# Second matmul of the channel MLP as seven block products (Strassen, Winograd's form) instead of eight, with the steps of all groups placed anew

## The chip, the cores and the metric

The kernel runs on one core of a Trainium2 chip. The metric is device time in microseconds. Three runs of the kernel before gave 284.55, 285.14 and 286.96 us; the median, 285.14, is the time before.

## The reference

Attention with pooled keys and values, then an MLP mixer with residuals, cut to its core:

```python
k_p = k.reshape(B, H, Sp, 8, D).mean(axis=3)          # B 8, H 8, S 576, D 64, Sp 72
v_p = v.reshape(B, H, Sp, 8, D).mean(axis=3)
attn = softmax(scale * q @ k_p.T)
x = (attn @ v_p) as (B, S, 512)
h = np.maximum(x.T @ w_tok1, 0.0) @ w_tok2            # tokens: 576 -> 256 -> 576
u = x + h.T
h2 = np.maximum(u @ w_ch1, 0.0) @ w_ch2               # channels: 512 -> 1536 -> 512
return u + h2                                         # float32
```

## The kernel before, in words

Five engines each work through a queue of their own in the order in which the program writes the instructions: TensorE (PE), VectorE (DVE), ScalarE (ACT), GpSimd (POOL), SyncE (SP, stores). Semaphores hold an instruction back until its data and its buffer are there; nothing else ties a queue to another.

**Groups.** The channel MLP is done in nine groups of 512 tokens. Groups 0 to 7 are the first 512 tokens of batches 0 to 7; group 8 is the remaining 64 tokens of all eight batches ("tails"). For one group `unit_steps` writes 12 hidden tiles m (4 matmuls of 512 columns each, L438, then a ReLU on ScalarE into GT, L442), and then 4 output tiles c (12 matmuls of 512 columns each, L461, then an addition of u on VectorE, L466, and two stores on SP, L469). In group 8 the last output tile is cut into two halves of 256 columns (L450, L453, L455). A `yield` after every two matmuls makes some 48 numbered steps of a group.

**The rest, woven in.** Attention and token mixing of the following batches are cut into small named pieces, and the tables FIRST, SECOND, THIRD and LATER (L476 to L488) say after which step of a group each piece is written. The pieces are those of batch n+1, with ">" of batch n+2, with "<" of batch n:

- K0, K1, V0, V1: pooling of half of the heads' keys or values on GpSimd; k0, k1, v0, v1: the same on VectorE. Each is `pool8` (L142), three additions of two SBUF tiles (L145, L146, then L149 for keys or L151 for values).
- lk, lq, lv: loads, issued by GpSimd. Q0 to Q3: transposes of q on VectorE (L243). kpT: four TensorE transposes of the pooled keys (L194) and a copy on VectorE (L196).
- s0 to s3: scores, 8 small matmuls (L254) and two exponentials on ScalarE (L260). av0 to av4: attention times values, 8 matmuls (L292), then a reciprocal and a product on VectorE (L304, L310).
- at0, at1: first token matmul, 5 matmuls (L338) and a ReLU on ScalarE or VectorE (L329, L331). u0 to u4: second token matmul, 2 or 4 matmuls (L353) and the addition of x on VectorE (L354).
- u must be transposed for the next group's hidden tiles: t0 to t4 do so on TensorE (L363, copy L364 on VectorE); M0, M2, M4, M and T0 to T4 do it through memory, by two DMA steps on SP (L372, L379) and a block transpose on VectorE (L385).

Batch 0 is prepared in a head (HEAD) ahead of group 0.

**PSUM.** Eight banks: three single ones (`ps_one`, "p1"), two double ones (`ps_two`, "p2", scores and av) and one for transposes (`ps_tr`, "pt"). A tile that takes over a bank waits for the readers of the one before.

## Time and profile before

| what | value |
|---|---|
| median of three runs | 285.14 us |
| span of the profiled execution, first to last instruction | 283.7 us (no other time of this execution is given) |
| end of HEAD, start of group 0 | about 24.7 us |
| group 0 | 24.7 to 63.4 us |
| groups 3, 4, 5 | 28.1, 29.0, 28.1 us |
| group 7, from the first hidden tile to the first of group 8 | 238.4 to 259.1 us |
| ReLU of a hidden tile, L442 | 0.596 us |
| output addition of 512 columns, L466 | 0.682 us |
| GpSimd busy, all ahead of 176 us | 138.1 us |

In the profile a line such as L438 is a line of the kernel; PEld is the loading of weights, which overlaps PE. In the chain of work that ended last, each piece is followed back to what released it; it tells which engine set the end. In the timeline, the columns are start, length, engine, line, operation and tiles, and in brackets the idle time of the engine ahead of it and what ended it. The granted clock of TensorE is 0.993 over the span; it is lower only in one slice of group 0.

### The profile page before, as it was taken

Reading aid. Unit: us, or ns where it says so; the run is one execution under the profiler, and the core shown is the slowest. Engines: PE = TensorE matmul, PEld = TensorE weight load, DVE = VectorE, ACT = ScalarE, POOL = GpSimd, SP = SyncE. Lnnn points to the kernel's source line nnn. Section 1 sums busy time; section 2 is a strip of 40 time slices with the busy share of each in tenths; the row PEclk is TensorE's granted clock in tenths of the full one; section 3 lists DMA queues with packets and bytes.
Section 4 is the critical chain, followed back from the end, with each engine's and each line's share of the span. In section 5 each row is a group of like instructions: output and inputs, shape, how many; then the busy total and the mean of one; then the engine's idle time right before and its main releaser. Section 6 shows DMA issues by size and latency. Waiting matters only on the chain.

```text
span 283.7 us, 4529 instructions
## 1 busy us (share of the span) xinstructions
PE 273.8 (97%) x1816; PEld 130.9 (46%) x1816; DVE 149.4 (53%) x279; ACT 110.2 (39%) x193; POOL 138.1 (49%) x124
## 2 busy tenths in 40 slices
PE   8999879999999999999999999999999999999994
PEld 3855325443544445354435443544354444444443
DVE  5466975679657557474648464746474243011012
ACT  2543554009602643514561356135613511612600
POOL 8684993999999929973993696000000000000000
PEclk9999979999999999999999999999999999999999
DMA  7999999951982397159748964514242346015014
GB/s 158 193 202 208 204 202 186 217 121 40 124 138 64 74 127 126 37 78 200 162 75 137 231 165 52 112 39 122 45 96 55 102 64 136 16 37 112 2 39 109
DMA packets 36837, 32.68 MB, mean 115 GB/s; under 512 B 14288, under 2 KB 30288, under 8 KB 36816
## 3 DMA queue, kind: packets, MB, share of 16 engines
q0 software_dynamic: 18672, 17.64, 40.0%
q1 hardware_dynamic: 17984, 14.62, 21.8%
q8 instruction: 14, 0.23, 0.3%
q10 hardware_dynamic: 160, 0.13, 0.2%
q14 instruction: 7, 0.06, 0.1%
HBM read 38.21 MB, written 11.80 MB: 176 GB/s over the span
## 4 chain that ended last, share of the span: by engine, by line
PE 91%; DVE 5%; ACT 2%; issue 1%
PE p L461 31%; PE p L438 31%; PE p L353 6%; PE p L338 5%; PE p L254 4%; PE p L292 3%; PE pt L495 3%; ACT ex L260 2%; DVE qD L243 1%; PE pt L363 1%; DVE t L145 1%; PE p L450 1%; PE p L272 1%; PE p L321 1%; PE p L403 1%; PE p L225 1%
## 5 line engine op out<-in xcount | busy, mean ns | idle before, releaser
L461 PE MATMUL p<-w_ch,GT 128*128 128x512 bf16 x420 | 102.3, 380 | 0.0
L442 ACT ACTIVATE GT<-p 128x512 bf16<-128x512 f32 x108 | 64.3, 596 | 80.6 <-PE p L438 80.5
L438 PE MATMUL p<-uT,w_ch 128*128 128x512 bf16 x384 | 95.5, 382 | 0.0
L438 PEld LDWEIGHTS <-w_ch 128*128 128x128 bf16 x432 | 40.2, 98 | 47.9 <-issue 4.8
L461 PEld LDWEIGHTS <-GT 128*128 128x128 bf16 x420 | 37.6, 98 | 41.2 <-issue 3.5
L260 ACT ACTIVATE ex<-p 72x576 bf16<-72x576 f32 x56 | 33.1, 642 | 28.4 <-PE p L254 28.4
L145 POOL TENSOR_TENSOR t<-kr 72x1024 f32<-72x1024 bf16 x13 | 27.5, 2118 | 26.6 <-DMA kr<-in_k_dram 25.9
L466 DVE TENSOR_TENSOR o<-p,u 128x512 f32<-128x512 f32 x32 | 21.8, 682 | 32.3 <-PE p L461 32.2
L146 POOL TENSOR_TENSOR t<-t 72x512 f32<-72x512 f32 x25 | 33.3, 1332 | 2.0
L354 DVE TENSOR_TENSOR u<-p,x 128x512 bf16<-128x512 f32 x32 | 22.1, 691 | 13.7 <-PE p L353 13.7
L145 POOL TENSOR_TENSOR t<-vr 72x1024 f32<-72x1024 bf16 x12 | 25.5, 2123 | 0.8
L385 DVE STREAM_TRANSPOSE uT<-v 128x512 bf16<-128x512 bf16 x16 | 10.4, 685 | 22.0 <-DMA v<-mem 22.0
L310 DVE TENSOR_TENSOR x<-p,den 128x512 bf16<-128x512 f32 x30 | 20.7, 692 | 1.0
L243 DVE STREAM_TRANSPOSE qD<-qb 128x576 bf16<-128x576 bf16 x28 | 20.5, 789 | 0.0
L329 ACT ACTIVATE AT<-p 128x512 bf16<-128x512 f32 x8 | 4.8, 597 | 39.3 <-PE p L338 36.6
L292 PEld LDWEIGHTS <-ex 72*128 72x128 bf16 x320 | 15.4, 98 | 9.9 <-DVE x L310 0.8
L353 PE MATMUL p<-AT,w_tok 128*128 128x512 bf16 x64 | 19.0, 379 | 0.0
L292 PE MATMUL p<-vp,ex 72*128 72x65 bf16 x320 | 16.8, 194 | 0.5 <-DVE x L310 0.3
L254 PE MATMUL p<-qD,kD 32*72 32x288 bf16 x224 | 14.5, 306 | 2.0 <-DVE kD L196 1.8
L304 DVE RECIPROCAL den<-p 128x8 f32<-128x8 f32 (+1 forms) x39 | 8.0, 204 | 13.6 <-PE p L292 13.0
L338 PE MATMUL p<-x,w_tok 128*128 128x512 bf16 x56 | 14.4, 380 | 0.0
L331 DVE TENSOR_SCALAR AT<-p 128x512 bf16<-128x512 f32 x8 | 5.5, 692 | 13.7 <-PE p L338 12.9
(88 smaller groups left out, 207.3 us busy)
## 6 DMA issues: line engine op xcount, KB each, us to landing
out_dram<-o SPq DMA_DIRECT2D x70, 128.0 KB, 2.4
kr<-in_k_dram POOLq DMA_DIRECT2D x7, 576.0 KB, 8.7
qb<-in_q_dram POOLq DMA_DIRECT2D x7, 576.0 KB, 11.9
vr<-in_v_dram POOLq DMA_DIRECT2D x7, 576.0 KB, 15.1
w_ch<-in_moe_w_ch_dram POOLq DMA_DIRECT2D x6, 512.0 KB, 13.2
mem<-u SPq DMA_DIRECT2D x8, 256.0 KB, 2.1
v<-mem SPq DMA_DIRECT2D x8, 160.0 KB, 3.7
v<-mem SPq DMA_DIRECT2D x8, 128.0 KB, 3.4
```

Of the source, the lines that this page charges most:

```text
L145: eng.tensor_tensor(out=t4[:, 0:n], in0=t[:, hs, 0:4], in1=t[:, hs, 4:8], op=ALU.add)
L146: eng.tensor_tensor(out=t4[:, 0:n, 0:2], in0=t4[:, 0:n, 0:2], in1=t4[:, 0:n, 2:4], op=ALU.add)
L243: nc.vector.transpose(out=late("qD")[:, g, db].rearrange("m (r j u) -> m u r j", u=2, r=BR), in_=st["qraw"][:, g].rearrange("m (u r d) -> ...
L254: nc.tensor.matmul(out=pss[l // 2][0:SP, l % 2, 0:SH], lhsT=st["kD"][quad, g, db, :], rhs=st["qD"][quad, g, db, half * SH:(half + 1) * SH] ...
L260: nc.scalar.activation(out=exv[:, h:h + 2], in_=pss[a][0:SP, :, 0:SH], func=AF.Exp, scale=scale)
L292: nc.tensor.matmul(out=halves[h // 4][:, (h % 4) * (D + 1):(h % 4 + 1) * (D + 1)], lhsT=st["ex"][:, h * S + n0:h * S + n0 + P], rhs=st["vp ...
L338: nc.tensor.matmul(out=ps, lhsT=w_tok1[:, c if c < 4 else 4 + par, m * P:(m + 1) * P], rhs=st["x"][:, c, :] if c < 4 else st["xt"], start= ...
L353: nc.tensor.matmul(out=ps, lhsT=w, rhs=a, start=(i == 0), stop=(i == len(mms) - 1))
L354: nc.vector.tensor_tensor(out=dst, in0=ps, in1=x, op=ALU.add)
L438: nc.tensor.matmul(out=ps, lhsT=w_ch1[:, kk, m * P:(m + 1) * P], rhs=uT[:, kk, :], start=(kk == 0), stop=(kk == 3))
L442: nc.scalar.activation(out=GT[:, m, :], in_=ps, func=AF.Relu)
L461: nc.tensor.matmul(out=ps, lhsT=GT[:, m, c * P:(c + 1) * P], rhs=w_ch2[:, m, :], start=(m == 0), stop=(m == NM - 1))
```

## The change

The second matmul of a group (512 tokens, 1536 hidden, 512 channels) is cut in two along each of its sizes: A11 to A22 of GT (a half of the tokens by a half of the hidden channels), B11 to B22 of w_ch2. It is computed from seven block products instead of eight. A product has 12 matmuls of 256 columns. Products 1, 2, 3 and 4 take at least one plain block, products 5, 6 and 7 take mixed ones: `S1` = A21 + A22, `S2` = S1 - A11, `S3` = A11 - A21, `S4` = A12 - S2 for the activations (`g_mix`, new in each group), and four mixes of the weights (`w_mix`, `W1` to `W4`, once, in group 0). They are written in the order 1, 2, 5, 6, 4, 3, 7. Products 1, 6 and 7 add up in one PSUM bank ("x"), 5 and 3 in another ("z"), 2 and then 4 each have one ("y"). Each of the four output quarters is read from two of these banks at different moments, by a first join (which adds u) and a second.

New names in the tables: S1 to S4 mix on VectorE and G1 to G4 on GpSimd ("a" and "b" mean the first and the second half of the hidden channels); C1a to C4b are joins on VectorE, D a drain of a bank to SBUF on ScalarE with E, the addition of u on GpSimd, in place of a first join. "=" means this group, "-" the one before, whose last joins run in the next group. Each group has a table of its own, and all pieces have new steps. New variants of pieces: kpA and r0 to r4 are kpT and t0 to t4 with the copy on ScalarE, aw0 to aw4 are av with the normalisation on ScalarE (eight instructions like L307), ax0 and ax1 are at with the ReLU on ScalarE; at0 now has it on VectorE.

A hidden group is written in the order of ORDER, so that both halves grow together. There are now 24 hidden steps and 21 product steps of four matmuls. PSUM has four single banks for all that was in `ps_one` and `ps_tr`. w_ch2 is loaded in four quarters, an output quarter is stored in two pieces with rows of 256 channels, and some tiles of the head share their SBUF with g_mix.

The diff, cut to its core:

```diff
-    ps_one = ctx.enter_context(tc.tile_pool(name="ps_one", bufs=3, space=bass.MemoryType.PSUM))
+    ps_one = ctx.enter_context(tc.tile_pool(name="ps_one", bufs=4, space=bass.MemoryType.PSUM))
     ps_two = ctx.enter_context(tc.tile_pool(name="ps_two", bufs=2, space=bass.MemoryType.PSUM))
-    ps_tr = ctx.enter_context(tc.tile_pool(name="ps_tr", bufs=1, space=bass.MemoryType.PSUM))
...
+    HM, HN, HT = NM // 2, DM // 2, 2 * P
+    w_mix = [w_ch2[:, 0:HM, HN:DM] if i == 2 else singles.tile([P, HM, HN], BF16, name=f"w_mix{i}") for i in range(4)]
+    g_mix = []
+
+    def early(i, shape, dtype):
+        return shared.tile(shape, dtype, name=f"shared{i}")
...
-    def load_ch2(gs):
-        for g in gs:
-            nc.gpsimd.dma_start(out=w_ch2[:, 4 * g:4 * g + 4, :],
-                                in_=moe_w_ch2[g * 512:(g + 1) * 512, :].rearrange("(c p) n -> p c n", p=P))
+    def load_ch2():
+        for j in range(2):
+            for i in range(2):
+                nc.gpsimd.dma_start(out=quad(w_ch2, i, j), in_=moe_w_ch2[i * HM * P:(i + 1) * HM * P, j * HN:(j + 1) * HN]
+                                    .rearrange("(c p) n -> p c n", p=P))
...
-        def kpT():
-            ps = ps_tr.tile([P, 4, SP], BF16, name="pt")
+        def kpT(eng):
+            def go():
+                transpose_keys(eng)
+            return go
+
+        def transpose_keys(eng):
+            ps = ps_one.tile([P, 4, SP], BF16, name="p1")
             for i in range(4):
                 nc.tensor.transpose(out=ps[:, i, :], in_=st["kp"][:, i // 2, i % 2].rearrange("j l d -> j (l d)"),
                                     identity=ident[0:SP, 0:SP])
-            nc.vector.tensor_copy(out=st["kD"].rearrange("p g e j -> p (g e j)"), in_=ps.rearrange("p i j -> p (i j)"))
+            eng(out=st["kD"].rearrange("p g e j -> p (g e j)"), in_=ps.rearrange("p i j -> p (i j)"))
...
+    def quad(t, i, j):
+        return t[:, i * HM:(i + 1) * HM, j * HN:(j + 1) * HN]
+
+    def mix_weights(i):
+        b11, b12, b21, b22 = quad(w_ch2, 0, 0), quad(w_ch2, 0, 1), quad(w_ch2, 1, 0), quad(w_ch2, 1, 1)
+        a, b = ((b12, b11), (b22, w_mix[0]), (b22, b12), (b21, w_mix[1]))[i]
+        nc.vector.tensor_tensor(out=w_mix[i], in0=a, in1=b, op=ALU.subtract)
...
+            self.bank, self.o = {}, {}
+            if not g_mix:
+                g_mix.extend(early(i, [P, HM, HT], BF16) for i in range(4))
...
+        def a(self, i, j):
+            return self.GT[:, j * HM:(j + 1) * HM, i * HT:(i + 1) * HT]
+
+        def mix(self, eng, i, m0, m1):
+            x, y, op = ((self.a(1, 0), self.a(1, 1), ALU.add), (g_mix[0], self.a(0, 0), ALU.subtract),
+                        (self.a(0, 0), self.a(1, 0), ALU.subtract), (self.a(0, 1), g_mix[1], ALU.subtract))[i]
+            eng.tensor_tensor(out=g_mix[i][:, m0:m1], in0=x[:, m0:m1], in1=y[:, m0:m1], op=op)
+
+        def product(self, i):
+            g, w, b = {1: (self.a(0, 0), quad(w_ch2, 0, 0), "x"), 2: (self.a(0, 1), quad(w_ch2, 1, 0), "y"),
+                       3: (g_mix[3], quad(w_ch2, 1, 1), "z"), 4: (self.a(1, 1), w_mix[3], "y"),
+                       5: (g_mix[0], w_mix[0], "z"), 6: (g_mix[1], w_mix[1], "x"), 7: (g_mix[2], w_mix[2], "x")}[i]
+            new = i in (1, 2, 4, 5)
+            if new:
+                self.bank[b] = ps_one.tile([P, 2, HN], FP32, name="p1")
+            ps = self.bank[b]
+            for k in range(2 * HM):
+                c, m = k // HM, k % HM
+                nc.tensor.matmul(out=ps[:, c, :], lhsT=g[:, m, c * P:(c + 1) * P], rhs=w[:, m, :],
+                                 start=new and k == 0, stop=k == 2 * HM - 1, skip_group_check=True)
+                if k % 4 == 3:
                     yield
...
+        def join(self, q, v, last):
+            u = self.uq(q // 2, q % 2)
+            if not last:
+                self.o[q] = outp.tile([P, 2, HN], FP32, name="o")
+            nc.vector.tensor_tensor(out=self.o[q], in0=self.bank[v], in1=self.o[q] if last else u, op=ALU.add)
+            if last:
+                self.store(q)
+
+        def drain(self, q, v):
+            self.o[q] = outp.tile([P, 2, HN], FP32, name="o")
+            nc.scalar.copy(out=self.o[q], in_=self.bank[v])
+
+        def add_u(self, q):
+            nc.gpsimd.tensor_tensor(out=self.o[q], in0=self.o[q], in1=self.uq(q // 2, q % 2), op=ALU.add)
+
+        def store(self, q):
...
+        def act(self, s):
+            v, g = nc.vector, nc.gpsimd
+            if s[0] == "S":
+                lo, hi = {"": (0, HM), "a": (0, HM // 2), "b": (HM // 2, HM)}[s[2:]]
+                self.mix(v, int(s[1]) - 1, lo, hi)
+            elif s[0] == "G":
+                lo, hi = {"": (0, HM), "a": (0, HM // 2), "b": (HM // 2, HM)}[s[2:]]
+                self.mix(g, int(s[1]) - 1, lo, hi)
+            elif s[0] in "CDE":
+                q, va, vb = {"1": (0, "x", "y"), "2": (1, "x", "z"), "3": (3, "z", "x"), "4": (2, "y", "x")}[s[1]]
+                if s[0] == "D":
+                    self.drain(q, va)
+                elif s[0] == "E":
+                    self.add_u(q)
+                else:
+                    self.join(q, vb if s[2] == "b" else va, s[2] == "b")
+
+    def unit_steps(n):
+        w = units[n] = Unit(n)
+        for m in ORDER:
+            yield from w.hidden(m)
+        for i in (1, 2, 5, 6, 4, 3, 7):
+            yield from w.product(i)
...
+    LAST = "C4a C2b C4b E3 C3b"
+    PLANS = [
+        {0: '<u1', 4: 'k1', 6: 'Q2 Q1 K0 Q0', 8: '<u0 <u3 Q3', 9: 'kpA s1 lv2', 11: 's0', 12: 'v0', 14: '=S1a s2', 16: 'V1 <u2', 17: 's3', 18: '=S2a', 19: 'lq3 W1', 20: 'av0', 21: 'av2', 22: 'av1', 23: '=G3 aw4 >K0', 24: '=S1b av3', 25: 'W2', 26: 'W3 W4 ax0 =D1 ax1', 27: 'u4 u2', 28: 'r4 =S2b =E1', 29: '=C1b u1', 31: 'u3', 32: 'r2', 33: '=S4', 34: 'r1', 35: 'lk3 =C3a u0', 36: '>Q2', 37: 'r3', 38: 'lv3 =D2 >K1', 39: '>V1', 40: '>kpA', 41: '>Q3', 42: 'r0 >s2'},
+        {0: '-C4a >Q3 -E2', 1: 'Q1 >Q1', 2: 'Q0', 3: '-C3b >Q2 s1 V0', 6: '-C4b', 8: 's0 -C2b', 9: 'lv3', 11: '>Q0', 12: 's3 >K1', 13: '>k0', 15: 'av1 lq3', 16: 'av2', 18: 'av0', 19: '=S1a >V1', 20: 'av4', 21: '>V0', 22: 'av3', 23: '=S1b =S2a >kpA', 24: 'at0 >s2', 26: '=C1a ax1 >s0', 27: 'u3', 28: 'u2', 29: '=G3 =S2b', 31: '>s3 =C1b', 32: '=C3a', 33: 'u1 u0', 34: '>s1 t1', 36: '=S4 =C2a', 38: '>av2', 39: 't2 =D4', 40: '>av3', 41: 'r0 r3', 42: '>aw1', 43: 'lk3'},
+        {0: '-C2b >K1 -E4', 2: 'av0', 4: 'av4', 5: '>K0 >Q1 -C3b', 7: '>Q0', 8: '-C4b lk3', 9: '>Q3', 11: 'ax1', 13: 'ax0', 14: '>kpA', 15: '=S1a >Q2', 16: 'u4', 17: '>s3', 18: 'u2', 19: 'lv3', 21: 'u0 u3 =S2a', 23: 'r2 >s0', 24: 't0', 25: 't3 =S1b', 26: 'u1 >s2 >V0', 27: 't4', 29: '=S2b', 30: '=C1a', 31: '>s1 =S3', 32: '=C1b', 33: '>V1', 34: '=C3a =G4', 35: '>aw1 >av4', 36: '=C2a t1', 41: 'lq3', 42: '=C4a >av2', 43: '>aw3'},
+        {2: '-C4b -C2b >Q3', 3: 'av0', 4: '>Q0', 6: '-C3b >Q1', 7: 'ax0', 8: 'at1', 10: '>K0 >Q2 >K1 >kpT', 12: 'u2', 14: 'u1 u0 u3', 15: '>s1', 17: 'lk3 >V0', 18: '=S1a', 19: 'M0 lq3', 24: 'M2 >s0 =S1b', 27: '=S2b M =S2a', 29: '>s3', 30: '=S4', 31: '>V1', 32: '=C1a =C1b', 33: '>s2 T2', 34: 'T0', 35: '=D2 T1', 36: '=C3a >aw3', 38: 'T3 >av1', 39: '=G3', 40: '=C4a lq4', 43: '>aw2'},
+        {0: '-C4b', 1: 'lv2', 2: '-C3b', 3: '>K0 av4 av0', 4: '-E2 >K1', 5: '>kpA >Q1', 7: '>Q2', 8: '>Q0 -C2b', 9: 'lk3 >Q3', 10: 'ax1 >s0 at0', 12: '=S1a >s1', 14: '=S2a', 15: '>V1', 16: 'u4', 17: 'u2', 18: '>s3 u1 lv3', 19: '>V0', 20: 'u3', 21: '>s2 u0', 25: '=S1b >aw1', 27: '=C1a M4 =S2b', 29: '>av3', 30: 'M2', 31: '>av0 =G4', 33: 'M0 M =D3 >aw2', 34: '=S3', 35: '=C1b', 36: '=D2', 38: '=E3 >av4', 40: '=E2 >ax0 T0', 41: 'T1', 42: 'T3', 43: 'T2 >ax1', 44: '=C4a'},
+        {1: '-C2b -C3b', 3: 'u0 >Q3', 7: '-C4b', 8: '>K1 u3', 9: '<T4 u2', 10: 'u1', 11: '>K0', 12: '>Q2', 13: '>kpA', 14: '>Q1 >V0', 17: 'M2 >V1', 19: '>s2', 20: '=S1a', 23: 'M0 >Q0', 24: '>s0 =S2a M =S1b', 28: '=S2b', 29: '=G4 >s1', 30: '=C1a', 31: 'T0 =S3', 32: '=C1b', 33: '>s3', 35: 'T2 =C3a', 36: '=D2', 37: '>aw1', 38: 'T3 T1', 41: '>av4', 43: '=C4a', 44: '=E2 >av2 =C2b'},
+        {2: 'av0', 5: '-C3b av3', 7: 'at1', 9: 'at0', 10: '-C4b', 14: 'u2', 15: 'u0 u3', 16: '=S1a', 18: 'u4 u1', 19: 'M2', 20: 'M4', 24: 'M0', 25: '=G3', 26: '=S2a', 27: '=S1b =S2b', 29: 'M =C1a', 30: '=C1b =G4', 32: '=C3a T2', 36: '=D2', 37: 'T1', 39: '=D4 T0 =E4', 40: '=E2', 43: 'T3'},
+        {0: '-C2b', 4: '-C3b', 10: '-C4b', 20: '=S1a', 24: '<T4', 27: '=S1b =C1a', 28: '=S2b', 31: '=S2a =G3', 33: '=C1b', 35: '=S4', 38: '=C3a', 40: '=D4', 41: '=C2a =E4'},
+        {3: '-C2b', 4: '-C4b', 5: '-C3b', 24: '=S1a', 26: '=S1b', 28: '=S2a', 32: '=S2b =D1 =E1', 33: '=D3 =C1b', 34: '=S4', 35: '=G3', 40: '=C2a'},
...
+    ORDER = (0, 6, 1, 7, 2, 8, 3, 9, 4, 10, 5, 11)
...
+        for n in range(B + 1):
+            unit(n, PLANS[n])
+        for s in LAST.split():
+            units[B].act(s)
```

## The prediction

> **What bounds the kernel now.** I read the page's busy shares first, then the chain that ended last, then the timeline around two places that the change touches.
>
> ```profile
> PE 273.8 (97%) x1816; PEld 130.9 (46%) x1816; DVE 149.4 (53%) x279; ACT 110.2 (39%) x193; POOL 138.1 (49%) x124
> ...
> PE 91%; DVE 5%; ACT 2%; issue 1%
> ```
>
> TensorE sets the time: it is busy for 97% of the span and holds 91% of the chain. VectorE, at 53%, seems to have room. The second matmul can be read in the pieces of the chain for the last two groups:
>
> ```profile
> 248.76 10.36 PE p L461 x48
> ...
> 277.25 2.63 PE p L450 x24
> ```
>
> 48 matmuls of 512 columns take 10.36 us, 215.8 ns each; 24 of 256 columns take 2.63 us, 109.6 ns each. So half the width costs half the time, and the doubled number of weight loads does not show.
>
> The second place is batch 1's key pooling, which VectorE and GpSimd do at the same time (VectorE's rows, then GpSimd's; columns are start, length, instruction):
>
> ```profile
> 29.21 2.73 DVE L145 TENSOR_TENSOR t<-kr 72x1024 f32<-72x1024 bf16 x1
> 31.98 1.64 DVE L146 TENSOR_TENSOR t<-t 72x512 f32<-72x512 f32 x1
> 33.65 0.83 DVE L149 TENSOR_TENSOR kp<-t 72x256 bf16<-72x256 f32 x1
> ```
> ```profile
> 28.75 2.11 POOL L145 TENSOR_TENSOR t<-kr 72x1024 f32<-72x1024 bf16 x1 [3.27 <-DMA kr<-in_k_dram]
> 30.94 2.13 POOL L146 TENSOR_TENSOR t<-t 72x512 f32<-72x512 f32 x1
> 33.15 1.05 POOL L149 TENSOR_TENSOR kp<-t 72x256 bf16<-72x256 f32 x1
> ```
>
> The ends tell it. GpSimd's first add ends at 30.86; VectorE's, which started at 29.21, ends 1.08 us after that, at 31.94. GpSimd's second add then takes 2.13 us instead of the 1.26 of the same form alone (37.25), and ends 1.13 us after VectorE's. **They take turns**: a VectorE instruction with two SBUF inputs lasts until GpSimd's current one is over and then runs for its own length, and the reverse. VectorE's instructions with a PSUM input keep their length beside GpSimd (0.69 us for L354 and L310 throughout). In before only nine VectorE instructions are of the first kind, all ahead of 71 us.
>
> **The change part by part.** The profile gives only the span of its execution, 283.7 us; the median of the runs is 285.14, so 1.4 us lie around it, and I add them at the end.
>
> *The products.* Each group has 84 matmuls of 256 columns instead of 48 of 512: 84 x 109.6 ns = 9.21 us for 10.36, 1.15 us less. The last group had 36 x 215.8 + 24 x 109.6 ns = 10.40 and loses 1.19. Eight groups and the last: **-10.4 us**. The other matmuls (hidden layer, tokens, attention, 14 transposes) keep their number.
>
> *What this is paid with.* Per group VectorE gets up to three full mixes (6 x 256 elements a row, some cut in half), and 8 joins for 4 (a few go to ScalarE and GpSimd); GpSimd gets one or two mixes and up to three adds. Once there are four weight mixes. A join reads PSUM, 0.69 us as L466. For a mix of two bf16 SBUF tiles before has no row. Bounds: f32 adds (0.42 us for 256, 0.69 for 512) lead to 0.96 us for a half mix and 1.76 for a full one; bf16 copies (0.295 for 288, 0.42 for 512, L196 and L364) lead to 0.56 and 0.99. I take the copies, the row of the same type, and keep the adds for the range. A GpSimd mix is 3.2 us (L145: 2.12 for 1024, same type).
>
> The Trainium skill, "VectorE: DVE Perf Modes", section on the perf-mode tiers, puts bf16 tensor_tensor in SBUF at two elements a cycle; the estimate by its 1224 ns for 2048 elements is about 0.56 us for a half mix, and by its f32 rate it would be 0.96; no row of before decides.
>
> By length alone VectorE goes from some 150 to 180 us, below the span. What counts is where the mixes stand: they are all of the kind that takes turns, and GpSimd is busy through group 5.
>
> *Order in the last groups, by group 7.* There is no attention left, so each wait is seen. Count from the first product (before has the same moment here):
>
> ```profile
> 247.93 0.60 ACT L442 ACTIVATE GT<-p 128x512 bf16<-128x512 f32 x1 [0.27 <-PE p L438]
> ...
> 248.59 2.75 PE L461 MATMUL p<-w_ch,GT 128*128 128x512 bf16 x12
> 248.79 0.60 ACT L442 ACTIVATE GT<-p 128x512 bf16<-128x512 f32 x1 [0.27 <-PE p L438]
> ```
>
> The last hidden tile but one is done at -0.06, the last at +0.8. G3 on GpSimd reads only tiles that are there at -0.06 and stands at the head of its queue, whatever its step says: it runs from 0 to 3.2. S1b needs the last tile, asks at 0.8 and lasts until 3.2 + 0.56 = 3.75. Product 5, due after 24 matmuls at 2.63, waits 1.15. Behind S1b on VectorE stand C1a (to 4.5), S2b (5.05) and S2a (5.6); product 6, now due at 5.1, waits for S2a, 0.55. Then C1b, S4 (0.99) and C3a, to 8.0; product 3, due at 6.97, adds to the bank that C3a reads and waits 1.1. Sum 2.8. Without turns all would be ready in time (S2a at 3.4, C3a at 5.8), so the price is the turns alone. Group 6, same count: S1b waits for G3, product 5 loses 1.2, the rest fits. Group 8: E1 waits for the ScalarE drain, so G3 is late and the mixes are through: 0.1. Group 3: GpSimd's V1 is done by about 15 us of the group, so G3 again meets S1b; S2b, S2a, S4 and C1a are queued behind it (all ahead of product 6): 1.7. Group 2, where S3 is behind G4 and the joins behind S3: 1.2; groups 4 and 5, where the queues fit: 0.5. **Together +7.5**, from 2 (G's late, or the turns broken up) to 13 (half mixes of 0.96).
>
> *Start of group 0.* Here before waits already:
>
> ```profile
> 34.25 0.52 PE L194 MATMUL pt<-ident,kp 72*128 72x72 bf16 x4 [0.86 <-POOL kp L149]
> 34.61 1.03 PE L438 MATMUL p<-uT,w_ch 128*128 128x512 bf16 x4
> 37.45 0.70 PE L254 MATMUL p<-qD,kD 32*72 32x288 bf16 x8 [1.82 <-DVE kD L196]
> ```
>
> Batch 1's keys are in SBUF at 28.7 and pooled at 34.5, and the change moves neither the load nor the pair of engines. But its key transposes go from step 14 to 9 and the first scores from 16 to 9. TensorE gets there at 24.85 + 10 x 0.43 + three u's (1.3) = 30.5, waits until 34.3, then for three q transposes behind the pooling on VectorE, until 36.65. Before it was at 37.45 with seven half tiles and one u more behind it, 3.46 us of work. 3.46 - 0.8 = **+2.7**. What follows the idle time is in both: four L438 took 1.89 us at 38.09 (granted clock 0.7 in that slice), for 0.86.
>
> *Rest of group 0.* VectorE has v0, W1 to W4, five mixes, joins, and all the normalisations and u's left at 36.6: some 22 us of its own length, to 59, plus turns: v0 (3.9 for 2.35 at 37.34 in before) and W2 to W4, S2b and S4 beside G3 and K0, K1: 6 to 10 more. TensorE's own rest ends at 62.9, and at 64.6 with the slow clock. Now VectorE is level with it or behind, and u's and joins hold PSUM banks: **+2.5**, from 0 to 6.
>
> *Group 1.* k0 stands on VectorE ahead of av1. In before this trio took 5.3 and 4.0 us beside GpSimd. av1 and av2 fill both two-bank tiles, so av0 waits: cover is five steps and two avs, 2.8 us. With the joins still queued: **+2**, from 0 to 4.
>
> *Transposes through memory.* On SP's queue the spills (M0, M2, M4) run as early as their u's allow, whatever step they have, 2.2 us apart. From the last spill to the first block transpose before took 7.7 to 9.2 us (193.77 to 201.45, 136.67 to 145.86), and four transposes take 2.6 to 3. Its T's ended 10 steps ahead of the next group; now they stand in the last ten. Group 6: its last u is at step 18, 13.6 us into the group, the spills leave until 16.9, the first T can start at 24.6 and the fourth ends at 27.4; the group's products end at 26.2, and group 7 waits 1.2. Group 3: T2, T0 and T1 are ahead of C3a and wait for the memory until 23, product 3 loses 0.4. Groups 4 and 5 have room. **+1.5**, from 0 to 3.
>
> *At nothing:* loads and stores (same bytes, in twice the pieces; the loads land long before use, and stores are behind the work, except the last), the bank that transposes had for themselves (four single banks now serve all; products hold three, and one is enough while VectorE is on time; else it is in the terms above), ScalarE (110 us busy, some 35 more: nine normalisations of 1.7 (L307), copies and drains).
>
> *Tail.* After the last matmul before has 0.42 us on VectorE; now C4b and C3b both wait for the last product, 1.38: **+1.0**.
>
> Sum: -10.4 + 7.5 + 2.7 + 2.5 + 2.0 + 1.5 + 1.0 = +6.8; 283.7 + 6.8 + 1.4 = **292 us**.
>
> The Trainium skill, "GPSIMD Engine Reference", section 1, says that GpSimd's SBUF interfaces are shared with VectorE where VectorE has two SBUF inputs. It names no price; the trace has one. Had I read only VectorE's 53%, without turns, the sum would be 282.4 (nothing in groups 2 to 8, 2 less in group 0).
>
> **Rivals.** *The gain arrives* (0.31, on the other side): GpSimd reaches the G's later than I count, or VectorE wins the first turn, so that mixes run alone. For it: without turns all of group 7 fits as worked out above. Against it: nothing but data holds GpSimd back, and its first add of a batch starts with the load's landing (28.75). 285.1 - 10.4 + 1.0 = 275.7; with the start of group 0, 278.4. *VectorE becomes the bound* (0.20), the worse side: mixes run at one element a cycle. 60 half mixes x 0.4 = 24 us more, of which 1.2 to 2 in each of groups 3, 6, 7 (S1b, S2b, S2a, S4 in a row), some 3 in groups 0 and 1 each: +8 to 10, 301. It decides from the point at which VectorE's own length and turns in group 0 or 1 pass TensorE's 32 us. *Half width does not pay*, weight loads showing: L450 at 109.6 ns excludes it.
>
> **How the numbers follow.** My forecast, 292, with its own 285 to 298, has 0.49; the gain 0.31; the bound 0.20. The bounds of the terms (2 to 13, 0 to 6, 0 to 4, 0 to 3) reach from 280 to 304; the gain reaches to 275.7. Leaving out a tenth on each side gives 276 to 302. A measurement tells 1% from no change: 282.3 and 288. Faster 0.31; same, the low part of my own case, 0.15; slower 0.54.
>
> **What would show it.** Right: half-width matmuls at 109 to 110 ns; TensorE idle from about 30.5 to 36.6; VectorE's mixes in groups 3, 6 and 7 ending 0.5 to 1 us after a GpSimd instruction, with a length of 2 us and more; TensorE waiting for g_mix. Wrong: mixes of 0.56 us beside GpSimd, or the groups 6 and 7 at 19.6 us plus what they carry of tokens. A store that ends late, or a bank held over a group's start, would be a cause that I have at nothing.

## The result and the profile after

The changed kernel takes 299.0 us (median of four runs, 297.66 to 299.32) where the kernel before, beside it, takes 284.85: 1.046 times as long, 95% interval 1.041 to 1.052. The profiled execution has a span of 297.6 us instead of 283.7, 13.9 more. The forecast was 292, with a range from 276 to 302: slower, and for a reason that is there, but half of the loss was not where the sum put it.

The page of the kernel after, busy shares and then the chain that ended last:

```profile
PE 264.1 (89%) x2103; PEld 161.0 (54%) x2128; DVE 213.5 (72%) x325; ACT 139.5 (47%) x293; POOL 188.8 (63%) x147
...
PE 61%; DVE 16%; DMA 13%; issue 4%; POOL 2%; ACT 1%; SPq 1%; DVEq 0%; POOLq 0%
```

TensorE is busy 9.7 us less than before (264.1 for 273.8), which is nearly the whole gain that was forecast for the products (10.4), but it fell from 91% of the chain to 61%. What came in is VectorE, 16%, and DMA, 13%; DMA had no share worth a percent in before, VectorE 5%. Not all of this is new time: 22.0 us of DMA's share are loads ahead of 29 us, which before has as well; the chain runs through them now because group 0 waits for the pooled keys. The pieces of that chain say where (start, length, what it is):

```profile
144.62 7.35 DMA mem<-u
153.80 10.12 DMA v<-mem
164.04 1.90 DVE uT L397 x3
...
240.72 2.70 DVE shared L481
...
281.26 5.25 PE p L493 x48
286.56 1.76 DVE shared L481
```

48 matmuls of half width take 5.25 us, 109.4 ns each, so the half width pays as it did in before. Two kinds of waits eat it: mixes (`shared` by L481) and, in group 3, a detour through memory of over 17 us. The waits of TensorE by what ended them (us in total, times, longest):

```profile
PE p L493 <- DVE o L506: 8.7, 2, 5.7
PE p L206 <- POOL kp L156: 4.1, 1, 4.1
PE p L375 <- DVE u_tails L366: 3.0, 1, 3.0
PE p L493 <- DVE shared L481: 2.3, 5, 0.5
...
PE p L375 <- DVE u L366: 1.2, 1, 1.2
```

The first line (products behind a join) is group 3 alone. Of its 5.7 us, ahead of product 6, TensorE waits 3.75 for the mix S2a (until 156.41) and then 1.9 for the join C1a behind it; the other 2.96 are ahead of product 3, for the join C3a. The second line is the start of group 0, the third and the last are u's of group 0 behind weight mixes and S4; the fourth is spread over groups 1, 6, 7 and 8. All idle time of TensorE together (neither matmul nor weight load, from its first instruction to its last) is 25.5 us, 4.9 in before. These 20.6 us more, 2.6 more behind the last matmul and 9.4 less in which TensorE works make up the 13.9, but for rounding.

A table by group shows the places. A group's length is counted from the first weight load of its hidden tiles to that of the next group's, in us; the last one ends with the span. By this count group 0 of before ends at 62.0, not at 63.4 as the table ahead of the prediction has it. The columns to the right are experiments told of below.

| group | before | after | no mixes (e8) | mended (e9) | e9, mixes on GpSimd (e12) | e9, group 0 plain (e11) |
|---|---|---|---|---|---|---|
| 0 | 37.4 | 47.0 | 39.3 | 43.8 | 45.1 | 38.5 |
| 1 | 32.9 | 30.6 | 29.9 | 30.1 | 30.6 | 31.8 |
| 2 | 32.3 | 29.9 | 29.0 | 29.0 | 30.0 | 29.0 |
| 3 | 28.1 | 36.9 | 34.2 | 26.5 | 32.7 | 26.5 |
| 4 | 29.0 | 30.3 | 30.3 | 32.3 | 30.9 | 32.3 |
| 5 | 28.1 | 24.6 | 24.6 | 24.6 | 24.6 | 24.6 |
| 6 | 25.6 | 25.6 | 25.0 | 25.2 | 25.6 | 25.2 |
| 7 | 20.7 | 20.8 | 19.4 | 19.4 | 20.8 | 19.4 |
| 8 and tail | 24.9 | 26.9 | 26.2 | 25.4 | 26.2 | 25.4 |

Groups 0 and 3 lose 9.6 and 8.8 us; the other seven together are 4.8 us shorter than before. Each column is one execution: group 0, written the same in after, e4 and e5, took 47.0, 45.9 and 46.7 us, so 1 us there means little.

**Group 3 as the trace has it.** VectorE's timeline in after, and GpSimd's beside it (start, length, instruction, in brackets the idle time ahead and what ended it):

```profile
148.49 2.68 DVE L481 TENSOR_TENSOR shared<-GT 128x768 bf16<-128x768 bf16 x1 [2.57 <-ACT GT L472]
151.28 5.12 DVE L481 TENSOR_TENSOR shared<-shared,GT 128x768 bf16<-128x768 bf16 x2
156.44 1.36 DVE L481 TENSOR_TENSOR shared<-GT,shared 128x1536 bf16<-128x1536 bf16 x1
157.73 0.68 DVE L506 TENSOR_TENSOR o<-p,u 128x512 f32<-128x512 f32 x1
158.51 0.69 DVE L506 TENSOR_TENSOR o<-p,o 128x512 f32<-128x512 f32 x1
164.04 1.30 DVE L397 STREAM_TRANSPOSE uT<-v 128x512 bf16<-128x512 bf16 x2 [4.84 <-DMA v<-mem]
```
```profile
147.67 3.09 POOL L481 TENSOR_TENSOR shared<-GT 128x1536 bf16<-128x1536 bf16 x1 [1.17 <-ACT GT L472]
150.71 0.75 POOL L109 DMA_DIRECT2D qb<-in_q_dram  x1
151.46 0.84 POOL L92 DMA_DIRECT2D vr<-in_v_dram  x1
152.32 2.13 POOL L152 TENSOR_TENSOR t<-kr 72x1024 f32<-72x1024 bf16 x1
154.53 1.46 POOL L153 TENSOR_TENSOR t<-t 72x512 f32<-72x512 f32 x1
```

Read the ends again. S1b (the half mix of 148.49) lasts until 151.18, 0.42 us after G3's end at 150.76, and takes 2.68 us where the same form alone takes 0.55. Then S2b and S2a stand in one row, 5.12 us for 1.1: behind G3 GpSimd had gone on into the next group's key pooling (L152, L153), and they took turns with that. The joins follow, at 157.73. Behind them three block transposes of u wait for the memory until 164.04, and the join that product 3 needs stands behind these three on VectorE.

### The profile page after: what moved, and what is told of

It reads as the page before. It is cut to its first block, busy times and chain, and to the rows that moved or that the text cites. A ratio compares the mean times of both kernels' runs of the same rounds, so it can differ in the third digit from the quotient of the medians.

```text
span 297.6 us, 5353 instructions
## 1 busy us (share of the span) xinstructions
PE 264.1 (89%) x2103; PEld 161.0 (54%) x2128; DVE 213.5 (72%) x325; ACT 139.5 (47%) x293; POOL 188.8 (63%) x147
## 4 chain that ended last, share of the span: by engine, by line
PE 61%; DVE 16%; DMA 13%; issue 4%; POOL 2%; ACT 1%; SPq 1%; DVEq 0%; POOLq 0%
PE p L468 26%; PE p L493 20%; PE p L365 5%; DMA kr<-in_k_dram 5%; PE p L350 5%; DVE shared L481 4%; DMA v<-mem 3%; DMA vr<-in_v_dram 3%; PE p L304 2%; DMA mem<-u 2%; PE p L266 2%; DVE qD L255 2%; DVE o L506 2%; DVE w_mix L451 1%; DVE t L153 1%
## 5 line engine op out<-in xcount | busy, mean ns | idle before, releaser
L468 PE MATMUL p<-uT,w_ch 128*128 128x512 bf16 x371 | 93.9, 385 | 1.0 <-ACT AT L341 0.2
L468 PEld LDWEIGHTS <-w_ch 128*128 128x128 bf16 x432 | 40.4, 99 | 46.7 <-issue 4.9
L493 PEld LDWEIGHTS <-shared 128*128 128x128 bf16 x432 | 41.1, 100 | 21.1 <-DVE shared L481 7.9
L481 DVE TENSOR_TENSOR shared<-GT 128x768 bf16<-128x768 bf16 (+1 forms) x21 | 27.7, 1321 | 23.5 <-ACT GT L472 23.4
L481 POOL TENSOR_TENSOR shared<-GT 128x1536 bf16<-128x1536 bf16 x6 | 18.5, 3089 | 35.4 <-ACT GT L472 35.4
L153 POOL TENSOR_TENSOR t<-t 72x512 f32<-72x512 f32 x25 | 35.3, 1410 | 2.0
L493 PE MATMUL p<-w_mix,shared 128*128 128x256 bf16 x216 | 29.7, 284 | 7.5 <-DVE o L506 5.7
L152 POOL TENSOR_TENSOR t<-kr 72x1024 f32<-72x1024 bf16 x12 | 25.8, 2151 | 7.2 <-DMA kr<-in_k_dram 7.0
L493 PE MATMUL p<-w_ch,shared 128*128 128x256 bf16 x216 | 27.0, 273 | 3.5 <-DVE o L506 3.0
L152 POOL TENSOR_TENSOR t<-vr 72x1024 f32<-72x1024 bf16 x13 | 28.1, 2159 | 0.5
L506 DVE TENSOR_TENSOR o<-p,o 128x512 f32<-128x512 f32 x36 | 23.8, 677 | 6.0 <-PE p L493 3.2
L493 PE MATMUL p<-w_ch,GT 128*128 128x256 bf16 x216 | 28.0, 276 | 0.0
L481 POOL TENSOR_TENSOR shared<-GT,shared 128x1536 bf16<-128x1536 bf16 x4 | 12.4, 3095 | 15.8 <-DVE shared L481 15.8
L319 ACT ACTIVATE x<-p,den 128x64 bf16<-128x64 f32 x72 | 15.7, 330 | 12.7 <-DVE den L316 12.6
L481 DVE TENSOR_TENSOR shared<-shared,GT 128x768 bf16<-128x768 bf16 x18 | 21.4, 1200 | 0.2
## 6 DMA issues: line engine op xcount, KB each, us to landing
vr<-in_v_dram POOLq DMA_DIRECT2D x7, 576.0 KB, 10.6
```

The costliest lines, as they stand in the source:

```text
L152: eng.tensor_tensor(out=t4[:, 0:n], in0=t[:, hs, 0:4], in1=t[:, hs, 4:8], op=ALU.add)
L153: eng.tensor_tensor(out=t4[:, 0:n, 0:2], in0=t4[:, 0:n, 0:2], in1=t4[:, 0:n, 2:4], op=ALU.add)
L319: nc.scalar.activation(out=dst[:, h * D:(h + 1) * D], in_=view[:, h // 4, h % 4, 0:D], func=AF.Copy, scale=den[rows, h // 4, h % 4:h % 4 + 1])
L468: nc.tensor.matmul(out=ps, lhsT=w_ch1[:, kk, m * P:(m + 1) * P], rhs=self.uT[:, kk, :], start=(kk == 0), stop=(kk == 3))
L481: eng.tensor_tensor(out=g_mix[i][:, m0:m1], in0=x[:, m0:m1], in1=y[:, m0:m1], op=op)
L493: nc.tensor.matmul(out=ps[:, c, :], lhsT=g[:, m, c * P:(c + 1) * P], rhs=w[:, m, :], start=new and k == 0, stop=k == 2 * HM - 1, skip_grou ...
```

## The experiments

Each kernel's ratio is to before on the same chip, with its 95% interval. Edits are shown against after, unless another run is named; pieces of the tables are shown alone.

### e1: pooling on GpSimd cut to a copy

In `pool8`, ahead of the three additions:

```diff
+        if eng is nc.gpsimd:
...
+                eng.tensor_copy(out=dst, in_=t[:, hs, 0])
+            return
```

> Left out: GpSimd's pooling of keys and values takes one of the eight rows instead of adding all eight, one copy of 256 elements (one SBUF input) instead of three additions; VectorE's own poolings, the mixes, the places of all steps and all TensorE work are as in the changed kernel. Theory of turns: VectorE's 43 us of additional length on instructions with two SBUF inputs fall to 10 to 16 (what the mixes and additions of u on GpSimd leave), W2 to W4 take about 1 us each, group 0 falls from 47.0 us to 38 to 41, and in group 3 the wait of product 6 (5.6 us) falls to 1 to 2, while the transposes through memory still end that group late; span 297.6 to 286 to 291. Rival, that VectorE is bound by its own length and by where the steps stand: the mixes keep their order and length without GpSimd beside them, the idle times of TensorE in groups 0 and 3 stay, span 295 to 298.

Measured: 279.3 us, ratio 0.982 (0.972 to 0.992). W2 to W4 take 0.95 us each instead of 1.91, 2.01 and 2.58; TensorE is idle for 10.6 us instead of 25.5, group 0 is at 38.5 and group 3 at 28.1. So what GpSimd does costs some 18 us, more than expected. But the run removes more than the turns: the pooled keys come earlier (the wait of 4.1 us for them is gone), and with its pooling short GpSimd also issues the loads sooner (the last one ahead of group 3's spill, that is the write of u to memory, at 120.37 instead of 141.25). On its own it would have led to putting all of group 3 down to turns.

### e2: the activations' mixes on VectorE

```diff
             elif s[0] == "G":
-                self.mix(g, int(s[1]) - 1, lo, hi)
+                self.mix(v, int(s[1]) - 1, lo, hi)
```

> The ten activation mixes that the changed kernel has on GpSimd go to VectorE, at the same steps; nothing else changes. Theory of turns: S1b no longer meets a GpSimd mix of 3.1 us, so TensorE's waits in the products of groups 6, 7 and 8 (1.0 to 1.3 us each) go, and S1b in group 3 takes 0.55 us instead of 2.68; against this VectorE gets 9.5 us more of its own, so groups 0 and 1 can lose 1 to 2; span 291 to 295. Rival, VectorE bound by its own length: 9.5 us more on the engine that is late make it slower, 299 to 303.

Measured: 291.6 us, ratio 1.024 (1.014 to 1.034). Added over all its instructions with two SBUF inputs, VectorE spends 46.6 us by their length alone (0.55 us for a half mix, 0.95 for a full one) and 22.9 us beyond it; in after it is 37.2 and 43.4. So 9.4 us of more work on VectorE made the kernel 7 us faster: it isn't VectorE's own length that sets the time, and the rival that would have had it slower fell. Group 7 is at 19.4. Group 3 still takes 34.8.

### e3: start of group 0 in the order of before

```diff
-  6: 'Q2 Q1 K0 Q0', 8: '<u0 <u3 Q3', 9: 'kpA s1 lv2', 11: 's0', 14: '=S1a s2', 16: 'V1 <u2', 17: 's3'
+  6: 'Q2 Q1 K0 Q0', 8: '<u0 <u3 Q3', 9: 'lv2', 14: 'kpA =S1a', 16: 's1 V1 <u2', 17: 's0', 18: 's2 =S2a', 19: 's3'
```

> In group 0 the key transposes go back from step 9 to 14 and the four scores from 9, 11, 14, 17 to 16, 17, 18, 19, as in the kernel before, with the attention products one to two steps later; all other tables stay. If the start costs what the prediction said (seven half tiles that wait behind the pooled keys): TensorE's idle time at 31 to 36.5 us falls from 5.1 to 2 to 3 us, and the span by 2 to 3 us, to about 295. Rival, that the rest of group 0 is set by VectorE anyway: TensorE only waits later (behind W2 to W4 and the normalisations), span 297 to 298.

Measured: 296.7 us, ratio 1.042 (1.028 to 1.056); group 0 at 45.6 us. The wait of 4.1 us for the pooled keys went, and this one stood in its place (TensorE's waits):

```profile
PE p L468 <- DVE u L366: 3.6, 1, 3.6
```

The u's of batch 0 are written behind k1 and the q transposes on VectorE; they hold PSUM banks that the hidden tiles need. The group is 1.4 us shorter than in after, little more than the 1.1 between equal groups. The start gives back what the forecast put on it only when the u's are moved as well, which e6 does.

### e4: group 3's joins ahead of its block transposes

```diff
-  33: '>s2 T2', 34: 'T0', 35: '=D2 T1', 36: '=C3a >aw3', 38: 'T3 >av1'
+  33: '>s2', 35: '=D2', 36: '=C3a >aw3', 38: 'T2 T0 T1 T3 >av1'
```

> In group 3 the block transposes T2, T0, T1 and T3 are written after the join C3a (steps 38 instead of 33 to 38). If product 3's wait of 2.96 us is C3a standing behind transposes whose data comes late from memory, the wait goes and the span falls by 2 to 3 us, to about 295, with TensorE now waiting at most 0.5 us for the transposes at the start of group 4. Rival, that late data is needed at the start of group 4 as well: the wait only moves there, span 297 to 298.

Measured: 296.6 us, ratio 1.043 (1.033 to 1.052). Group 3 went from 36.9 to 34.9: of the two waits for a join, 8.7 us, one of 5.7 is left, at product 6. The block transposes no longer hold the join, but the mixes still do.

### e5: the last stores on two queues

```diff
-                    nc.sync.dma_start(out=dst, in_=src)
+                    (nc.scalar if half else nc.sync).dma_start(out=dst, in_=src)
```

> The second half of each output quarter is stored from ScalarE's queue in the last group instead of SyncE's. In after SyncE issues six store pieces one after another, about 0.65 us apart, from 290.66 to 294.60, and the end is 6.4 us behind the last matmul (3.8 in before). Theory (the tail is set by one queue that issues six pieces): three pieces on each queue, the last one issued some 1.5 us sooner, the end some 4.9 us behind the last matmul, the ratio to before about 1.040. Rival (the landing of the last piece sets it, or the drain on ScalarE is delayed by the issues): the end stays 6 us or more behind the last matmul.

Measured: 298.0 us, ratio 1.044 (1.036 to 1.052). The last store is issued at 291.91 instead of 293.98, and the end comes 5.6 us behind the last matmul instead of 6.4: half of the expected gain. Of the 1.8 us that remain to before's 3.8, some 0.9 are the two joins that both wait for the last product (1.29 us for 0.42); the rest wasn't followed.

### e6: the mends together

e2, e4 and e5, and the start of group 0 with its u's where before had them:

```diff
-  0: '<u1', 4: 'k1', 6: 'Q2 Q1 K0 Q0', 8: '<u0 <u3 Q3', 9: 'kpA s1 lv2', 11: 's0',
+  0: '<u0', 1: '<u1', 2: '<u2', 3: '<u3', 4: 'k1', 6: 'Q0 Q1 K0 Q2', 8: 'Q3', 9: 'lv2',
...
-  14: '=S1a s2', 16: 'V1 <u2', 17: 's3'
+  14: 'kpA =S1a', 16: 's1 V1', 17: 's0', 18: 's2 =S2a'
```

> Mixes of activations on VectorE, group 3's joins ahead of its block transposes, the last stores on two queues, and the start of group 0 in the order of before, u0 to u3 included, so that no u stands behind k1 on VectorE. Theory (each loss has its own cause): from 291.6 (mixes on VectorE) 2 for the tail, 3 for group 3, 3 to 5 for the start of group 0: 281 to 284, level with before or a little faster. Rival (group 0 is set by VectorE's sum of work beside GpSimd, whatever the order at its start): group 0 stays at 45 us and the time at 286 to 288, slower than before.

Measured: 290.2 us, ratio 1.017 (1.011 to 1.024), some 7 us worse than expected. Group 0 went from 46.2 in e2 to 43.5, so the start was worth 2.7 us. But group 3 stayed at 34.8, with all mixes short. VectorE's timeline there:

```profile
143.71 0.56 DVE L481 TENSOR_TENSOR shared<-GT 128x768 bf16<-128x768 bf16 x1 [3.32 <-ACT GT L472]
144.31 1.03 DVE L481 TENSOR_TENSOR shared<-shared,GT 128x768 bf16<-128x768 bf16 x2
...
153.94 2.49 DVE L397 STREAM_TRANSPOSE uT<-v 128x512 bf16<-128x512 bf16 x4 [3.28 <-DMA v<-mem]
...
157.16 2.49 DVE L481 TENSOR_TENSOR shared<-GT 128x1536 bf16<-128x1536 bf16 x1
```

S1b, S2b and S2a take their own length now, 0.56 and 1.03 for two. Then the block transposes wait for the memory, and S3, which stands behind them in the queue and which product 7 needs, comes at 157.16 and lasts 2.49 us (0.95 alone): one wait of 6.8 us. The turns had hidden the second cause.

### e7: less pooling on VectorE

Against e6, first in group 0, then in group 1:

```diff
-  12: 'v0'
+  12: 'V0'
...
-  13: '>k0'
+  13: '>K0'
```

> As the sum of mends, and batch 1's second half of values (group 0) and batch 2's second half of keys (group 1) pooled on GpSimd instead of VectorE. Takes some 5 us of VectorE with two SBUF inputs out of each of the two groups and adds as much to GpSimd. Theory (VectorE's length and turns set group 0): group 0 shorter by 1 to 3 us than in the sum of mends. Rival (GpSimd's longer row moves the turns into the mixes of the following groups, groups 2 and 3 above all): group 0 shorter, but groups 1 to 4 longer by as much, time unchanged.

Measured: 296.4 us, ratio 1.040 (1.032 to 1.048), 6 us worse than e6. Group 0 is longer, not shorter (45.2 for 43.5), group 2 too (33.4 for 29.0): GpSimd's longer row delivers pooled values late (2.5 us of wait for `vp` at 43.6) and reaches into the mixes of the next groups. Both the theory and the rival had group 0 shorter.

### e8: all mixes left out

```diff
-            eng.tensor_tensor(out=g_mix[i][:, m0:m1], in0=x[:, m0:m1], in1=y[:, m0:m1], op=op)
+            pass
```
(the same for w_mix; products 3 to 7 take plain blocks)

> All mixes are left out, of the weights and of the activations; the products take plain blocks instead, so the output isn't the reference's. Products, joins, order of steps, banks, loads and stores are as in after. Theory (turns between VectorE's mixes and GpSimd cost most of the difference): the products of groups 3, 6, 7 and 8 don't wait for VectorE any more, groups 6 and 7 at 24.5 and 19.6 us, group 3 at 28 to 30, group 0 at 41 to 43, the time 279 to 283, ratio 0.98 to 0.99. Rival (the new order of steps, the joins and the shared banks cost it): the time stays above 290, with the idle time in the same places.

Measured: 284.6 us, ratio 0.996 (0.992 to 1.000). So the mixes cost 14.6 us of span (297.6 to 283.0): 7.7 in group 0, 2.7 in group 3, 1.4 in group 7, less elsewhere. And even with mixes that cost nothing the kernel would be level with before: what else came with the change (the steps' new places, more joins, the longer tail) uses up the 10.4 us of the products. Most of that is group 3, which was expected at 28 to 30 and is at 34.2, with no mix in it (VectorE's timeline):

```profile
150.10 1.90 DVE L397 STREAM_TRANSPOSE uT<-v 128x512 bf16<-128x512 bf16 x3 [7.61 <-DMA v<-mem]
151.92 0.65 DVE L506 TENSOR_TENSOR o<-p,u 128x512 f32<-128x512 f32 x1
```

### e9: two loads behind the spill

Against e6: GpSimd issues batch 7's queries and batch 6's values behind group 3's addition of u (E2) instead of ahead of it, and S3 stands ahead of the block transposes (first group 3's table, then group 4's).

```diff
-  36: '=C3a >aw3', 38: 'T2 T0 T1 T3 >av1', 39: '=G3', 40: '=C4a lq4'
+  36: '=C3a >aw3', 37: '=G3', 38: 'T2 T0 T1 T3 >av1', 40: '=C4a'
...
-  0: '-C4b', 1: 'lv2', 2: '-C3b', 3: '>K0 av4 av0', 4: '-E2 >K1'
+  0: '-C4b', 2: '-C3b', 3: '>K0 av4 av0', 4: '-E2 lv2 >K1 lq3'
```

> As the sum of mends, and two loads of 576 KB (batch 7's queries, batch 6's values), which GpSimd issues at 136.23 and 136.98 there, are written behind group 3's addition of u on GpSimd (150.50), so that u's spill at 139.24 and 139.84 meets one load instead of three; S3 stands ahead of the block transposes on VectorE. Theory (the spill waits for the loads in flight: 1.66 MB at about 200 GB/s are 8.3 us, and 9.05 to 9.65 were measured from spill to read): from the last spill to its read 2.1 to 4.5 us instead of 9.05, the first block transpose by about 148 instead of 153.9, no wait of 6.84 us at product 7's neighbours in group 3, group 3 at 28 to 29 us instead of 34.8, the time 283 to 285. Rival (the spill's delay is the memory round trip of this stage, whatever is in flight): read still 9 us behind, group 3 at 34 us.

Measured: 281.6 us, ratio 0.985 (0.979 to 0.991): 1.5% faster than before. Group 3 went from 34.8 to 26.5. SP's queue in e6 and in e9, spills (L384) and reads (L391), from the trace:

```profile
139.24 0.98 SPq L384 DMA_DIRECT2D mem<-u  x2
148.89 1.93 SPq L391 DMA_DIRECT2D v<-mem  x4
```
```profile
139.93 0.98 SPq L384 DMA_DIRECT2D mem<-u  x2
143.01 2.73 SPq L391 DMA_DIRECT2D v<-mem  x4
```

The read follows as soon as the spill has landed: 9.65 us after the first spill's issue in e6, 3.1 us in e9. That it is the loads, and not this stage, is seen by comparing runs (times of issue, in us):

| run | last load ahead of the spill | last spill | read | spill to read | load to spill |
|---|---|---|---|---|---|
| before | 124.88 | 136.67 | 140.88 | 4.2 | 11.8 |
| e1 | 120.37 | 135.58 | 137.97 | 2.4 | 15.2 |
| e9 | 131.83 | 140.53 | 143.01 | 2.5 | 8.7 |
| e11 | 127.57 | 136.28 | 140.92 | 4.6 | 8.7 |
| after | 141.25 | 144.62 | 152.02 | 7.4 | 3.4 |
| e12 | 139.54 | 142.92 | 150.52 | 7.6 | 3.4 |
| e6 | 136.98 | 139.84 | 148.89 | 9.1 | 2.9 |
| e8 | 132.47 | 135.45 | 145.34 | 9.9 | 3.0 |

With a load of 576 KB issued 3.4 us or less ahead of it, the spill takes 7.4 to 9.9 us (6.8 to 9.6 in e2, e3, e4, e5 and e7, which aren't in the table); with 8.7 us or more, 2.4 to 4.6. Why it takes 2.5 in e9 and 4.6 in e11 at the same distance isn't shown. Between 140 and 149 us in e6 the DMA engines are busy for a mean of 82%. In after the reads met two more loads (150.71 and 151.46): from the last read at 153.80 to the first block transpose are 10.2 us, 3.3 to 3.6 in before, e6 and e8.

The Trainium skill, "DMA: Bandwidth & Descriptors", section on queues, rings and completion order, says that each DMA engine goes round between the queues that have work for it, a packet at a time. A spill on SP's queue would then share the engines with GpSimd's loads instead of passing them. The table agrees with that; no run shows the order of the packets.

e9 does not divide the 8.3 us between its two edits. The loads' move makes the spill early, as the table shows; S3's place takes an urgent mix out from behind the transposes. An estimate from e6's lines: the loads alone would save the 3.28 us in which VectorE waits ahead of the transposes; S3's place alone would spare product 7 the wait, but the transposes would still end at 156.4, some 2 us behind the moment at which group 4 could start, and so it would save 4 to 6. A late spill costs only where something that TensorE needs stands behind the transposes on VectorE: a join in after and e8, S3 in e6. With nothing there it is harmless, as e4 and e12 show.

### e10 and e11: the first group with plain products

Against e9: group 0 computes eight plain products, each output quarter with 24 matmuls of 256 columns in one bank and one join, and the weights' mixes stand behind them.

```diff
+        if n == 0:
+            for q in (0, 1, 3, 2):
+                yield from w.plain(q)
+            return
         for i in (1, 2, 5, 6, 4, 3, 7):
             yield from w.product(i)
```

> As the run with the loads behind the spill, and group 0 computes its second matmul as eight plain products (each output quarter in one bank, one join), the four mixes of the weights move behind them. Takes the mixes of the activations and four joins out of the group in which VectorE and GpSimd have most to do, adds 1.3 us of matmuls. Theory (group 0's excess is VectorE's queue, its own length and its turns): group 0 from 43.5 us to 38 to 40, the time 278 to 281, 1.5 to 3% faster than before. Rival (the key pooling at its start and the late u's set it): group 0 at 42 or more, the time 284 to 286.

Measured: four times, from 279.4 to 543.1 us, too far apart for a ratio. In the longest one the matmuls alone were longer (L468 672 ns each for 379 in e11), at a granted clock of 1.0; weight loads and the other engines kept their lengths. The trace doesn't show the reason. The second run of the same kernel, e11:

> The kernel of the run with the first group plain once more, since its times lay far apart (279.41 to 543.1, one execution with every matmul at twice its length) and give no comparison. Theory as there: group 0 at 38 to 40 us instead of 43.8, the time 277 to 281. Rival: group 0 at 42 or more, the time no better than 281.

Measured: 280.4 us, ratio 0.982 (0.974 to 0.989). Group 0 took 38.5 us for 43.8, as the theory said, with 12 matmuls more. So most of its excess came with the mixes and joins; what of it is VectorE's own length and what are turns, the run doesn't divide. Group 1 gave 1.7 of it back (31.8 for 30.1, with a wait of 1.9 us for a transpose of q). The gain over e9 by the medians is 1.2 us, within the intervals; the span is 277.6 for 281.8.

### e12: the mixes back on GpSimd

Against e9, the edit of e2 undone.

```diff
-                self.mix(v, int(s[1]) - 1, lo, hi)
+                self.mix(g, int(s[1]) - 1, lo, hi)
```

> As the run with the loads behind the spill, with the mixes G1 to G4 on GpSimd again, as in after: what the turns cost once the late spill no longer covers them. Theory (turns): in groups 3, 6, 7 and 8 S1b takes 2.5 us and more beside G3, product 5 and product 6 wait; group 3 at 29 to 31 us instead of 26.5, groups 6 and 7 at 25.6 and 20.8 instead of 25.2 and 19.4, the time 4 to 7 us above 281.6. Rival (what was measured as turns in group 3 was the late spill's wait alone): group 3 at 26.5 to 27.5, the time 1 to 3 us above.

Measured: 291.9 us, ratio 1.022 (1.015 to 1.029), a span of 291.5 for e9's 281.8. VectorE's S1b, S2b and S2a of group 3, in e9 and then in e12:

```profile
144.40 0.56 DVE L481 TENSOR_TENSOR shared<-GT 128x768 bf16<-128x768 bf16 x1 [3.43 <-ACT GT L472]
144.99 1.03 DVE L481 TENSOR_TENSOR shared<-shared,GT 128x768 bf16<-128x768 bf16 x2
```
```profile
146.79 2.68 DVE L481 TENSOR_TENSOR shared<-GT 128x768 bf16<-128x768 bf16 x1 [2.57 <-ACT GT L472]
149.58 3.82 DVE L481 TENSOR_TENSOR shared<-shared,GT 128x768 bf16<-128x768 bf16 x2
```

Groups 6 and 7 are at 25.6 and 20.8 as in after. Group 3 is at 32.7, worse than the theory's 29 to 31, and far from the rival's 27. The spill is late again here too (7.6 us: GpSimd's queue is later by the mixes, and its load meets the spill), but nothing waits for it: the block transposes stand behind the joins and go at 159.75, with their data there.

Group 3 then has a table of its own, mixes by transposes. In e4 the transposes are as late as in after, but TensorE waits for nothing behind them, so it stands to the right:

| | TensorE waits behind transposes held by a late spill | it doesn't |
|---|---|---|
| G3 on GpSimd, turns | 36.9 (after) | 32.7 (e12), 34.9 (e4) |
| G3 on VectorE, or no mixes | 34.8 (e6), 34.2 (e8) | 26.5 (e9) |

Each cause alone costs 6 to 8 us, both together 10: they lie beside each other, so that taking either away from after shows 2 to 4 us of it.

## Why the prediction was right, and where it was wrong

**The direction and the mechanism.** Slower, because VectorE's two-SBUF-input instructions and GpSimd's take turns. That holds: mixes alone 0.55 and 0.95 us, beside GpSimd up to 3.6; over all mixes in after 30.4 us by length and 35.6 us in turns. e2 (more work on VectorE, 7 us faster) and e12 (the one edit, 9.7 us of span) show it without other changes. The rival that made VectorE's own length the bound rested on mixes at one element a cycle; 768 elements in 0.55 us and 1536 in 0.95 leave 1.9 a ns between them. This agrees with the two elements a cycle of the Trainium skill, "VectorE: DVE Perf Modes", section on the perf-mode tiers, which the forecast weighed.

**Products, -10.4.** Right: 109.4 ns, and TensorE is busy 9.7 us less with the same other matmuls.

**Turns in groups 2 to 8, +7.5.** By e12 less e9, with the same order of steps, they are 8.4 us (1.0, 6.2, -1.4, 0, 0.4, 1.4, 0.8 in groups 2 to 8). The sum is right by luck of places. In group 3, counted at 1.7, the working stopped at G3; GpSimd went on into the next group's pooling, and S2b and S2a took turns with that too. In group 7, counted at 2.8, product 5 could start on the first half of its mix and product 3 came late enough for its join: 1.4. In group 8, counted at 0.1, S4 met G3 after all (285.08 to 288.31).

**Start of group 0, +2.7.** Right in place, TensorE waits from 30.9 for the pooled keys and gets the first scores at 36.47 (36.65 was worked out), and right in size as far as single executions tell: TensorE idles 5.1 us there for 2.7 in before, and e6 against e2 got back 2.7 of the group. What it takes to get it back was not foreseen (e3).

**Rest of group 0, +2.5: mis-sized.** The group lost 9.6 us; less the start's 2.7, plus the products' 1.15, that is 8. Without mixes (e8) the group is 7.7 shorter, with plain products (e11 against e9) 5.3. The step compared VectorE's whole work with TensorE's at the group's end and took the difference. But TensorE waits for single pieces inside the row: the sum of a queue can fit while each u is late. Behind the start these waits are 5.4 us, and the matmuls after them are slower (granted clock 0.89 over the group, 0.95 in before). VectorE in after:

```profile
52.00 1.91 DVE L451 TENSOR_TENSOR w_mix<-w_ch,w_mix 128x1536 bf16<-128x1536 bf16 x1
53.83 2.01 DVE L451 TENSOR_TENSOR w_ch<-w_ch 128x1536 bf16<-128x1536 bf16 x1
55.77 2.58 DVE L451 TENSOR_TENSOR w_mix<-w_ch,w_mix 128x1536 bf16<-128x1536 bf16 x1
58.28 0.68 DVE L366 TENSOR_TENSOR u_tails<-p,xt 128x512 bf16<-128x512 f32 x1
```

Three weight mixes that nothing needs for several us stand ahead of a u whose transposes TensorE waits for, 3.0 us.

**Group 1, +2.** k0 took 5.7 us beside GpSimd (5.3 in before), but TensorE never waited for it: 0. The group is 2.3 shorter than before.

**Transposes through memory, +1.5, and loads at nothing: the step that failed.** Group 3 was put at 0.4, by 7.7 to 9.2 us from last spill to first block transpose as before had it; in after it is 19.4. The duration was taken from rows in which the last load had been issued 11.8 us or more ahead of the spill, and the loads were struck out because "the loads land long before use". They do; but they were moved too, onto the spill. By e9 against e6 that is 8.3 us where it is not hidden by the turns (S3's place is in that number, by the estimate at least half of it), and 4.2 by after against e12, where it partly is. Group 6, put at 1.2, lost nothing: its detour took 7.9 us, within the forecast's 7.7 to 9.2, but its last spill was issued 14.6 us into the group and not at 16.9.

**Tail, +1.0: mis-sized.** It is 2.6 (6.4 us behind the last matmul, 3.8 before). The two joins were seen; that SP issues the last six pieces one after another, 0.64 to 0.7 us apart, until 293.98 was not. Two queues give 0.8 back (e5).

Put together, the forecast had +6.8 of span, and +13.9 was measured; rest of group 0 and group 3's spill, 5.5 and some 4, and 1.6 of the tail make up more than the difference, the 2 and 1.2 that did not come in groups 1 and 6 stand against it. These terms overlap and don't add up exactly.

The forecast's other side, "the gain arrives" at 275.7 to 278.4, is 2 us below what e11 has (280.4, span 277.6), with group 3's two causes and the mixes of group 0 out of the way.

## What to carry to other kernels

When work is moved to VectorE, price it by the moments at which GpSimd is busy, and look at what GpSimd does *after* the piece that one has in mind, since nothing but its own queue holds it back. When steps are moved, list the DMAs by queue order and ask of each short, urgent transfer which long ones will be in flight beside it; a duration taken from a trace holds only for the company that it had there. Two delays that lie beside each other hide one another: a table of both, each with and without, shows what no single removal does.

## What the runs showed of the hardware

- A VectorE instruction with two SBUF inputs and a GpSimd addition alternate as wholes: a half mix (0.55 us alone) that begins during a GpSimd addition takes from 0.6 to 2.8 us, by how much of that one is left. In after there are 17 of these, and all end 0.41 to 0.43 us after the addition. GpSimd's own adds lengthen as well (L153 1.26 us alone, 1.86 beside VectorE's mixes).
- Some half mixes took longer than one turn explains (3.59 us at 151.28 in after, 3.52 at 54.76 in e6). Each began while GpSimd was issuing a load, with an addition directly behind the issue, and ended 0.43 us after that addition, as the others do after the one in which they begin. Over all runs there are ten such mixes, of 2.72 to 3.59 us, all ending 0.42 to 0.43 us after the addition. Seven that also began during an issue, but with GpSimd idle or only a copy (e1) behind it, took 0.54 to 0.65 us.
- The second of the two spills of 256 KB in group 3 took 2.4 to 4.6 us when the last load had been issued 8.7 us or more ahead, and 6.8 to 9.9 when it was 3.4 us or less.
- Behind waits of several us TensorE can run slower for a while. In after the granted clock is 0.50 for 6.8 us from 35.2 and for 3.4 us from 59.1 and from 158.1, at the ends of stretches with 5.1, 3.0 and 5.7 us of idle time; behind the wait of 3.0 us at 163.6 it stays at 1.00. Over the span it is 0.972, 0.993 in before. So a wait can cost more than its length.
